# The first weight load gated on one quad's V, and a new order of the steps, in a fused chunk-select attention and feed-forward kernel

## The chip, the cores and the metric

The kernel runs on one core of one Trainium2 chip. Its time is the device time of one execution in microseconds (us), lower is better. A core has TensorE (PE; its weight loads are listed apart as PEld), VectorE (DVE), ScalarE (ACT), GpSimd (POOL) and SyncE (SP, which here only issues DMAs). Each engine runs its own instructions strictly in the order in which the program lists them; they wait for one another through semaphores.

## The reference

Sizes: batch 4, 8 heads, 768 positions, head dimension 64; then 3072 tokens of width 512 into a hidden width of 2048. Cut to what matters:

```python
def _attn_ref(q, k, v):
    # chunks of 32 keys; top 6 chunks per query, causal
    k_min, k_max = k_chunks.min(axis=3), k_chunks.max(axis=3)
    ub = sum(maximum(q * k_min, q * k_max), axis=-1)        # per query and chunk
    ub = where(causal, ub, -1e9)
    top_chunks = argsort(ub)[..., -6:]
    scores = scale * (q @ k.T)
    scores = where(key's chunk in top_chunks and key <= query, scores, -1e9)
    return softmax(scores) @ v

def _moe_ref(x, w_in, w_out):
    h = x @ w_in
    g = h * clip(h + 3, 0, 6) / 6
    return g @ w_out
```

## The kernel before

**Tiling.** The heads go in pairs: p0 to p15, four pairs to a batch, two pairs to a quad. Quad 0 of batch 0 is p0 and p1, quad 1 is p2 and p3. A unit is a quad and a half of the 768 queries: u0 (quad 0, first half), u1 (quad 1, first half), u2 and u3 (the second halves) for batch 0; u4 to u7 for batch 1, and so on. When all four pairs of a batch have a half done, that half (384 tokens, a group: g00, g01, g10, ...) goes through the feed-forward part.

**Steps of a unit.** `turn` brings K and Q of a pair to a layout with the head dimension on partitions: on PE for batch 0 (L418, with `turn_out` that evicts it, L291 on ACT or L293 on DVE), on DVE for later batches (L430). `limits` takes maximum and minimum of each chunk on DVE (L443, L444) and their difference on POOL or DVE (L446). `bounds` multiplies them with the queries on PE (L499, tile UBT). On DVE follow `bounds_in` (L503), `largest` (L515), `select` (L520, L523) and `select_out` (L528, tile MT: the mask). `scores` (PE, L556 in batch 0, L559 later, tile SPS), `exponentials` (ACT, L569, tile PT), `triangle` (POOL, L574), `values` (PE, L590, tile PVP) and `values_out` (DVE, L596 and L602, tile Xb) are the attention proper. `cast_values` turns V into bf16 (tile VB from VS).

**Steps of a group.** `turn_tokens` (PE, L611) and `turn_tokens_out` (DVE, L615) for batch 0; then 16 times `hidden` (PE, L647, four matmuls of 384 columns from WIN into HP), `hidden_relu` (ACT, L652) and `hidden_out` (DVE, L655); then three times four `result` steps (PE, L662, four matmuls of 512 columns from WOUT into OP), `result_scale` and the store. Parts 0 and 1 of a result read the first half of WOUT, parts 2 and 3 the second. The last result of the kernel is split (L671). A hidden, a bounds or a result takes one of four PSUM banks (kind "m").

**Loads.** Q, K and V of batch 0 come by SP in pieces (`load_quad`, L266; `load_quad_values(n, part)`, L281, three parts for each of the units 0 to 3, into VS: units 0 and 2 hold quad 0's V, units 1 and 3 quad 1's). Batch 1's K and Q come as four pieces each (`load`, L275). The weights come by POOL in four pieces of 1 MB in bf16, in this order: WIN first half, WIN second half, WOUT first half, WOUT second half (L359, L362). Ahead of each, POOL copies a few elements of another tile ("seen", L356), which makes it wait until that tile has landed: the first for V, the second for the first half of WIN, the third for K of unit 4, the fourth for the second half of WIN.

**Order.** `Plan` holds all 1666 steps (an instruction group on one engine, or a DMA's landing), with lengths and dependencies. `ORDER` is a written-out list that gives each step a rank. `Plan.order` replays the steps with its own lengths, and whenever an engine is free it takes the ready step of lowest rank for which there is room; that yields each engine's program order. Steps that may run on two or three engines go to the one that would finish them sooner. Where the replay sees PE idle over 0.3 us in the first 45 us, it puts dummy matmuls ahead of the next step (L243).

Of the kernel before, what the change touches and what calls it, by code (L numbers as in the profile page):

```python
# [24 lines left out]


ORDER = [int(n) for n in """
# [43 lines left out]
""".split()]  # L71


# [126 lines left out]
def kernel(  # L200
# [575 lines left out]
    landing = {}  # L776
# [172 lines left out]
    for what in ("I0", "I1", "O0", "O1"):  # L949
        name, n = dict(I="WIN", O="WOUT")[what[0]], int(what[1])  # L950
        if what == "I0":
            got, seen = sum([landing["V%d" % i][0] for i in range(4)], []), lambda: VS[0:1, :, :, 3, 0]
        else:
            got, seen = landing[GATE[what]]
            got = got[-1:]
# [96 lines left out]
```

## Time and profile before

| | |
|---|---|
| median of 3 runs | 264.02 us (263.66 to 264.3) |
| profiled execution, own time | 264.45 us |
| its span (first to last instruction) | 262.7 us |
| time outside the span | 1.75 us |
| PE busy in the span | 257.8 us (98%) |
| DVE, ACT, POOL busy | 199.8, 186.5, 133.7 us |

The span starts at 0; all times of events below count from there. Busy time of an engine is the union of its instructions' durations; matmuls overlap in the pipeline, so the distance between starts, not the duration of one, tells how fast they are fed. A bracket at the end of a timeline row gives the engine's idle time before it and what ended it.

### The profile page before, as it was taken

Reading aid. Unit: us, or ns where it says so; the run is one execution under the profiler, and the core shown is the slowest. Engines: PE = TensorE matmul, PEld = TensorE weight load, DVE = VectorE, ACT = ScalarE, POOL = GpSimd, SP = SyncE. Lnnn points to the kernel's source line nnn. Section 1 sums busy time; section 2 is a strip of 40 time slices with the busy share of each in tenths; the row PEclk is TensorE's granted clock in tenths of the full one; section 3 lists DMA queues with packets and bytes.
Section 4 is the critical chain, followed back from the end, with each engine's and each line's share of the span. In section 5 each row is a group of like instructions: output and inputs, shape, how many; then the busy total and the mean of one; then the engine's idle time right before and its main releaser. Section 6 shows DMA issues by size and latency. Waiting matters only on the chain.

```text
span 262.7 us, 6919 instructions
## 1 busy us (share of the span) xinstructions
PE 257.8 (98%) x2544; PEld 157.1 (60%) x2544; DVE 199.8 (76%) x569; ACT 186.5 (71%) x310; POOL 133.7 (51%) x307
## 2 busy tenths in 40 slices
PE   8999999999999999999999999999999999999995
PEld 7865666664545676654666566544665576545543
DVE  5999898999998899989996999879584136804710
ACT  4599889794646799962999768823998297806812
POOL 6538699714956788692762999702533121200000
PEclk9999999999999999999999999999999999999999
DMA  7998999998738899935999993204403021302112
GB/s 205 326 216 125 194 158 216 137 183 154 204 100 161 178 202 144 244 111 157 176 183 209 198 222 145 60 2 116 125 20 105 0 80 48 117 2 80 40 42 80
DMA packets 117986, 35.91 MB, mean 137 GB/s; under 512 B 101184, under 2 KB 113728, under 8 KB 117952
## 3 DMA queue, kind: packets, MB, share of 16 engines
q1 hardware_dynamic: 114400, 30.98, 52.5%
q0 software_dynamic: 3136, 4.19, 10.2%
q8 instruction: 20, 0.33, 0.5%
q10 hardware_dynamic: 416, 0.30, 0.3%
q14 instruction: 14, 0.11, 0.1%
HBM read 29.23 MB, written 8.26 MB: 143 GB/s over the span
## 4 chain that ended last, share of the span: by engine, by line
PE 90%; DVE 6%; ACT 1%; DMA 1%; issue 1%; ACTq 0%; DVEq 0%
PE HP L647 32%; PE OP L662 30%; PE SPS L559 11%; PE PVP L590 8%; PE UBT L499 3%; PE SPS L556 2%; PE KT L418 1%; PE OP L671 1%; ACT PT L569 1%; DMA KS<-in_k_dram 1%; DVE KMA L443 1%; DVE KMA L444 1%; DVE T L515 1%; DVE MT L528 1%; PE QT L418 1%
## 5 line engine op out<-in xcount | busy, mean ns | idle before, releaser
L569 ACT ACTIVATE PT<-SPS 128x1024 bf16<-128x1024 f32 (+2 forms) x96 | 85.6, 935 | 21.7 <-PE SPS L559 18.8
L647 PE MATMUL HP<-XT,WIN 128*128 128x384 bf16 x512 | 90.7, 326 | 0.0
L655 DVE SCALAR_TENSOR_TENSOR GT<-U,HP 128x384 bf16<-128x384 bf16 x128 | 67.6, 548 | 24.9 <-ACT U L652 20.2
L662 PE MATMUL OP<-WOUT,GT 128*128 128x512 bf16 x368 | 85.7, 379 | 0.0
L652 ACT ACTIVATE U<-HP,THREE 128x384 bf16<-128x384 f32 x128 | 72.7, 600 | 12.0 <-PE HP L647 7.9
L647 PEld LDWEIGHTS <-WIN 128*128 128x128 bf16 x512 | 48.4, 98 | 30.1 <-issue 0.8
L662 PEld LDWEIGHTS <-GT 128*128 128x128 bf16 x368 | 35.0, 98 | 38.8 <-issue 2.2
L574 POOL TENSOR_SCALAR_AFFINE_SELECT PT<-PT 128x256 bf16<-128x256 bf16 x96 | 38.4, 410 | 37.1 <-ACT PT L569 35.7
L559 PE MATMUL SPS<-QLA,KL 128*128 128x384 bf16 (+2 forms) x240 | 35.8, 278 | 0.0
L374 POOL TENSOR_SCALAR_AFFINE_SELECT QLA<-QF 64x384 bf16<-64x384 f32 x48 | 24.1, 506 | 19.8 <-PE SPS L559 13.2
L689 ACT ACTIVATE OT<-OP 128x512 f32<-128x512 f32 x22 | 13.1, 597 | 25.1 <-PE OP L662 24.9
L559 PEld LDWEIGHTS <-KL 128*128 128x128 bf16 x240 | 21.6, 98 | 12.8 <-issue 0.5
L374 POOL TENSOR_SCALAR_AFFINE_SELECT KL<-KF 64x384 bf16<-64x384 f32 x48 | 24.1, 504 | 9.9 <-DVE KF L430 8.0
L590 PEld LDWEIGHTS <-PT 128*128 128x128 bf16 x672 | 24.0, 97 | 4.3 <-issue 0.6
L590 PE MATMUL PVP<-VB,PT 128*128 128x65 bf16 x672 | 25.6, 193 | 0.0
L602 DVE TENSOR_TENSOR Xb<-PVP,RINV 128x384 bf16<-128x384 f32 x32 | 18.5, 579 | 1.1
L596 DVE RECIPROCAL RINV<-PVP 128x6 f32<-128x6 f32 x32 | 5.8, 182 | 15.8 <-PE PVP L590 15.8
L640 POOL COPY XT<-BF 128x384 bf16<-128x384 bf16 x20 | 9.4, 509 | 15.6 <-DMA BF<-BD 15.3
L457 ACT ACTIVATE QR<-QF 128x384 f32<-128x384 f32 (+1 forms) x28 | 13.1, 489 | 5.9 <-DVE QF L430 5.8
L430 DVE STREAM_TRANSPOSE QF<-QS 128x384 f32<-128x384 f32 x24 | 12.9, 558 | 1.2 <-PE UBT L499 1.2
L443 DVE TENSOR_REDUCE KMA<-KF 128x12 f32<-128x384 f32 x24 | 13.0, 542 | 0.3
L444 DVE TENSOR_REDUCE KMA<-KF 128x12 f32<-128x384 f32 x24 | 13.0, 543 | 0.0
(81 smaller groups left out, 237.2 us busy)
## 6 DMA issues: line engine op xcount, KB each, us to landing
KS<-in_k_dram SPq DMA_DIRECT2D x31, 192.0 KB, 3.9
QS<-in_q_dram SPq DMA_DIRECT2D x31, 192.0 KB, 4.0
out_dram<-OT SPq DMA_DIRECT2D x20, 256.0 KB, 2.6
VT<-in_v_dram SPq DMA_DIRECT2D x24, 192.0 KB, 3.6
QLA<-MT SPq DMA_DIRECT2D x22, 96.0 KB, 2.2
WIN<-in_moe_w_in_dram POOLq DMA_DIRECT2D x2, 1024.0 KB, 9.6
WOUT<-in_moe_w_out_dram POOLq DMA_DIRECT2D x2, 1024.0 KB, 12.4
BD<-BT SPq DMA_DIRECT2D x5, 384.0 KB, 2.3
```

Of the source, the lines that this page charges most:

```text
L374: nc.gpsimd.affine_select(out=to, in_=x, pattern=[[0, n]], compare_op=A.is_ge, fill=0.0, base=0, channel_multiplier=0)
L443: nc.vector.tensor_reduce(out=over, in_=chunks, axis=X_AXIS, op=A.max)
L444: nc.vector.tensor_reduce(out=low, in_=chunks, axis=X_AXIS, op=A.min)
L559: nc.tensor.matmul(SP[:, j, c0:c0 + n], lhsT=KLS[st["pair"] % 6][:, j, jb * P:(jb + 1) * P], rhs=st["QL", half][:, j, at:at + n], start=Tr ...
L569: nc.scalar.activation(PT[:, :, 0:cols], SP[:, :, 0:cols], ACT.Exp, scale=scale)
L574: nc.gpsimd.affine_select(out=PT[:, :, c0:c0 + P], in_=PT[:, :, c0:c0 + P], pattern=[[0, 2], [1, P]], compare_op=A.is_ge, fill=0.0, base=0 ...
L590: nc.tensor.matmul(PVP[:, j, n, :], lhsT=PT[:, j, c0:c0 + P], rhs=st["VB"][:, jb, j, :], start=(jb == 0), stop=(jb == qb))
L602: nc.vector.tensor_tensor(out=to, in0=PVP[:, :, :, 0:D], in1=RINV[:].to_broadcast([P, 2, HB, D]), op=A.mult)
L647: nc.tensor.matmul(HP[:], lhsT=WIN[:, kt, f * P:(f + 1) * P], rhs=g["XT"][:, kt, :, :], start=(kt == 0), stop=(kt == KT_HID - 1))
L652: nc.scalar.activation(U[:], g["HP", f][:], ACT.Relu, bias=THREE[:], scale=1.0)
L655: nc.vector.scalar_tensor_tensor(out=g["GT"][:, f, :], in0=g["U", f][:], scalar=6.0, in1=g["HP", f][:], op0=A.min, op1=A.mult)
L662: nc.tensor.matmul(g["OP", t][:], lhsT=g["GT"][:, f, t * P:(t + 1) * P], rhs=WOUT[:, f, :], start=(f == 0), stop=(f == FT - 1))
```

## The change

The gate of the first weight load: it waited for all twelve landings of V of batch 0 and read one element of each of the twelve pieces; now it waits for the six landings of quad 1's V (units 1 and 3) and reads six elements. And `ORDER` is replaced by another permutation of the same 1666 steps. The steps themselves, their instructions, their sizes, `SEQ`, the other gates and the replay are the same.

```diff
 ORDER = [int(n) for n in """
-0 21 1 17 2 31 57 58 3 5 53 59 56 54 25 55 4 7 22 67 9 60 63 18 61 11 68 32 69 13 62 6 71 15 64 167 66 65 26 70 19 169 72 8 171 168 73 23 76 10 33 170 74 75 12 80 35 172
-77 174 14 47 173 16 84 49 81 93 78 43 94 85 95 186 79 96 20 97 86 82 24 83 88 194 37 87 34 39 98 91 187 36 89 177 51 90 191 48 99 190 41 175 195 50 27 199 178 115 92 44
...
+0 21 1 17 2 5 57 58 3 47 53 59 56 54 23 55 4 7 22 67 9 60 63 18 61 11 68 6 69 13 62 48 71 19 64 167 66 65 24 70 15 169 72 8 171 168 73 25 76 10 37 170 74 75 12 80 172 39
+77 173 14 49 174 20 78 27 81 93 84 31 94 79 95 186 83 96 16 85 88 82 175 187 26 86 43 191 190 38 176 51 177 97 89 40 87 29 179 194 50 90 91 33 98 178 28 195 180 45 92 182
...
         if what == "I0":
-            got, seen = sum([landing["V%d" % i][0] for i in range(4)], []), lambda: VS[0:1, :, :, 3, 0]
+            got, seen = landing["V1"][0] + landing["V3"][0], lambda: VS[0:1, 1, :, 3, 0]
```

Read with the steps' names, the places in the list (0 to 1665) of the steps that the prediction speaks of are:

| step | engine | place before | place after |
|---|---|---|---|
| last of quad 1's V loads, `load_quad_values(1,2)` | SP | 111, 23rd issue | 95, 20th issue |
| first and last of `load_quad_values(0,..)` | SP | 5, 56 | 69, 113 |
| `load_quad_values(2,2)` | SP | 100 | 117, the last of batch 0 |
| first half of WIN | POOL | 159 | 142 |
| second half of WIN | POOL | 227 | 225 |
| first half of WOUT | POOL | 250 | 289 |
| second half of WOUT | POOL | 338 | 353 |
| `bounds(u2)` | PE | 135 | 125 |
| `limits(p2,1)`, `limits(p3,1)` | DVE | 143, 182 | 165, 174 |
| `values_out(p0,0)` | DVE | 163 | 183 |
| `select_out(u2)` | DVE | 177 | 158 |
| `scores(p0,1,0)` | PE | 187 | 179 |
| `bounds(u3)` | PE | 196 | 195 |
| first `hidden` of g00 | PE | 248 | 247 |
| `triangle(p2,1,3)` | POOL | 288 | 287 |
| `values_out(p2,1)` | DVE | 305 | 310 |
| `turn(p4,QS,0)`, `turn(p5,QS,0)` | DVE | 354, 367 | 314, 320 |
| first step that reads the second half of WOUT | PE | 419, `result(g00,2,2)`, after 86 PE steps | 427, `result(g00,1,2)`, after 87 PE steps |

The 45 PE steps up to and with the two `turn_tokens` of g00 and the two scores behind them are the same set in both lists; only their order among themselves differs.

## Rows read from the trace of the kernel before

**Rows 1.** Page, part 1: busy us and share of the span, by engine.
```profile
PE 257.8 (98%) x2544; PEld 157.1 (60%) x2544; DVE 199.8 (76%) x569; ACT 186.5 (71%) x310; POOL 133.7 (51%) x307
```

**Rows 2.** Windows: stretch, its length, then busy us and instructions by engine, clock, DMA.
```profile
10.00:20.00 10.00, 10.00 (x156) 6.92 (x152) 9.62 (x38) 7.98 (x17) 3.78 (x11) 1.00 1.02 238
20.00:30.00 10.00, 9.37 (x146) 5.35 (x146) 8.80 (x41) 9.04 (x15) 7.41 (x17) 1.00 0.98 157
30.00:40.00 10.00, 9.58 (x154) 6.61 (x150) 9.75 (x22) 8.70 (x12) 8.82 (x20) 1.00 1.07 168
```

**Rows 3.** Chain that ended last, in order of time: start, us, what.
```profile
49.89 10.40 PE HP L647 x64
60.29 3.45 PE OP L662 x16
...
256.39 3.51 PE OP L671 x32
```

**Rows 4.** Timeline of PE, 22 to 36 us: start, us, what, idle before.
```profile
22.46 0.61 PE L243 MATMUL KT<-IDENTB 128*128 128x128 bf16 x8
...
25.78 0.34 PE L556 MATMUL SPS<-MT,EB 64*128 64x384 bf16 x2 [0.57 <-DVE MT L528]
...
26.76 0.85 PE L499 MATMUL UBT<-QF,KMA 64*32 64x384 f32 x8
...
30.56 0.34 PE L556 MATMUL SPS<-MT,EB 64*128 64x384 bf16 x2 [0.30 <-ACT PT L569]
...
35.41 0.82 PE L647 MATMUL HP<-XT,WIN 128*128 128x384 bf16 x4
```

**Rows 5.** Timeline of DVE, 21 to 51 us.
```profile
21.14 0.54 DVE L444 TENSOR_REDUCE KMA<-KT 128x12 f32<-128x384 f32 x1
...
23.38 0.56 DVE L602 TENSOR_TENSOR Xb<-PVP,RINV 128x384 bf16<-128x384 f32 x1
...
25.15 0.58 DVE L528 STREAM_TRANSPOSE MT<-SELA 128x384 bf16<-128x384 bf16 x1
...
28.32 0.58 DVE L503 STREAM_TRANSPOSE UB<-UBT 128x384 f32<-128x384 f32 x1 [0.99 <-PE UBT L499]
...
43.47 0.56 DVE L602 TENSOR_TENSOR Xb<-PVP,RINV 128x384 bf16<-128x384 f32 x1
...
50.90 0.57 DVE L430 STREAM_TRANSPOSE QF<-QS 128x384 f32<-128x384 f32 x1
```

**Rows 6.** Timeline of POOL, 20 to 49 us.
```profile
20.02 0.78 POOL L574 TENSOR_SCALAR_AFFINE_SELECT PT<-PT 128x256 bf16<-128x256 bf16 x2 [0.50 <-ACT PT L569]
...
21.95 0.19 POOL L356 COPY seenWIN<-VS 1x12 f32<-1x12 f32 x1
22.50 1.00 POOL L359 DMA_DIRECT2D WIN<-in_moe_w_in_dram  x1 [0.37 <-issue]
...
35.62 0.91 POOL L362 DMA_DIRECT2D WOUT<-in_moe_w_out_dram  x1
...
41.22 0.40 POOL L574 TENSOR_SCALAR_AFFINE_SELECT PT<-PT 128x256 bf16<-128x256 bf16 x1
...
48.95 0.93 POOL L362 DMA_DIRECT2D WOUT<-in_moe_w_out_dram  x1
```

**Rows 7.** Tiles VS (15.6 us) and QS (32.6 us): issue in ns, us to landing.
```profile
L281 SPq DMA_DIRECT2D VS<-in_v_dram x1: 770/770/770, 15.6 to 15.6; - x1
...
DMA to landing us min/median/max: 5.1/5.1/5.1
...
L275 SPq DMA_DIRECT2D QS<-in_q_dram x1: 857/857/857, 32.6 to 32.6; - x1
...
DMA to landing us min/median/max: 13.0/13.0/13.0
```

**Rows 8.** Tile WIN, 22 to 24 us: landing of the first half.
```profile
DMA to landing us min/median/max: 9.8/9.8/9.8
```

**Rows 9.** Tile WOUT, 48.9 to 50 us: landing of the second half.
```profile
DMA to landing us min/median/max: 12.0/12.0/12.0
```

82 rows, old and new, of the table ORDER are left out of this document.

## The prediction

> **What bounds the kernel now.** I read the page first: PE is busy for 98% of the span, far above the other engines [rows 1]. Matmuls overlap, so that share alone proves little, and I went on to the chain that ended last. From 49.89 us it shows 64 matmuls of HP in 10.40 us, 162 ns apiece, and 16 of OP in 3.45 us, 216 ns apiece [rows 3]. Single HP steps elsewhere in the timeline run at the same distance, so this is PE's own pace and not that of a feeder. The first HP is at 35.41 [rows 4]; from there on there is always feed-forward work to put between attention steps. The last matmuls start at 256.39 and last 3.51 [rows 3], so PE is done at 259.9 of 262.7; the 2.8 us behind it are the last eviction and store, and the change leaves these steps as they are.
>
> A change that alters no step can therefore act in two ways. It can let PE reach its first HP sooner, because the steps that PE does before that are the same set in both lists: the gain is idle PE time removed. Or it can open gaps behind 35.41, where there are hardly any to close. So the gain has a ceiling, which the windows give: PE has 0.63 idle from 20 to 30 us and 0.42 from 30 to 40 [rows 2], and it runs eight dummy matmuls of 0.61 [rows 4], in all 1.66 us. Before 20 us I count nothing: PE's first eight steps keep their places, and from 10 to 20 us PE is busy throughout [rows 2].
>
> **The Trainium skill on this reading.** The page "Perfetto Trace Analysis", section "Identifying the Most-Contended Engine", says that matmul busy share is a poor measure for TensorE and that the weight loads' busy share should be taken. That would be 60% [rows 1], which would leave some 100 us in which a better order could gain anywhere in the kernel. The 162 and 216 ns above speak against that room, so I give it no case.
>
> **The gate.** The first half of WIN is issued at 22.50, behind its copy at 21.95 [rows 6]. The last V landed at 15.6 + 5.1 = 20.7 [rows 7], so it isn't V that holds the copy in the end but POOL's queue: a triangle, a cast and a limit stand ahead of it. With the gate on quad 1, whose last load is now issued three places earlier, at 0.5 to 0.77 per issue [rows 7], V would allow the copy at some 18.4 to 19.2; but the copy still stands behind the triangles of p1, which ran at 20.02 to 20.80 [rows 6]. I expect the issue at 21 to 22, so 1.0 us earlier. The bounds are 0 (the queue decides alone) and 3.5 (21.95 against 18.4, V alone decides). What is that worth? WIN landed at 22.5 + 9.8 = 32.3 [rows 6, 8], and its first reader starts at 35.41. That is 3.1 us of slack, so the gate by itself is worth 0 in either case; the cover is the attention work of batch 0, and if the attention were ready before 32.3 it would be worth up to 1.0. The copy reads six elements instead of twelve: 0.19 us at most, on an engine with slack, 0 on the path.
>
> The Trainium skill's "DMA: Bandwidth & Descriptors", "Rules for kernel authors", advises issuing a DMA early and waiting late. By that rule the first HP would move with the load and give 1.0 us; the row above has it wait for something else, and I take 0.
>
> **The order, before the first HP.** Follow the mask of u2. PE waits 0.57 for it at 25.78 [rows 4], after DVE wrote MT at 25.15 [rows 5], and the dummies before that are also time in which PE had nothing useful. On DVE two things stood ahead of that mask: `limits(p2,1)`, two reductions of 0.54 that overlap a little, 1.0 in all, and `values_out(p0,0)`, 0.56 and a short reciprocal, 0.7 in all [rows 5]. Both are now behind `select_out(u2)`, and `bounds(u2)` stands ahead of the PE steps that it followed. So MT should come about 1.7 us earlier, at some 24.0 in place of 25.7 for its end, and PE needn't wait there.
>
> What is late next is `bounds(u3)`, which needs the limits of p3. DVE goes from 24.0 through `limits(p2,1)` and `limits(p3,1)`, 2 x 1.0, to 26.0, and POOL's difference takes some 0.35 with its semaphore: 26.35. Before, it started at 26.76 [rows 4]. That is 0.41 us gained. DVE's idle 0.99 at 28.32, while it waits for that step [rows 5], is then partly filled by the moved `values_out`. Behind it PE waits 0.30 for ACT [rows 4], and the windows leave about as much in small gaps up to 40 us. The exponentials of p0's second half can now start some 1.5 us sooner, so I take half of these 0.7, 0.35. The sum is 0.41 + 0.35 = 0.76, rounded to 0.75. Its bounds are 0 (ACT, at 9.04 of 10 us in this stretch [rows 2], was as binding as DVE) and the ceiling 1.66.
>
> Against its own time: the span goes from 262.7 to 261.95, and with the 1.75 us outside it from 264.45 to 263.7. That execution lies 0.43 above the median of the runs, 264.02, to which I apply the same difference: 263.3.
>
> V of quad 0 is now loaded among the last, so it lands about where quad 1's last did, at 20.7, or an issue later, 21.5. Its casts feed `values(p0,0)`, which stood just before the dummies of 22.46 [rows 4] and goes behind p3's scores, to about 23.6. That leaves 2 us for the casts, one instruction per pair and half, so I cost it at 0; without that cover PE would wait some tenths.
>
> **The order, after the first HP.** WOUT's first half is issued later: it was at 35.62, and now follows the triangle that ran at 41.22 [rows 6], so about 40.9. Its first reader is at about 60; with the 12.0 us that WOUT's second half took [rows 9] it lands at 53, hidden by some 7 us of PE's work. The second half goes behind three `queries` steps of about 0.53 and loses one or two steps ahead of it: net some 0.5 later on POOL, less the 0.75 gained. I keep 49 for the issue and 61.0 for the landing [rows 6, 9]. Its first reader came two result steps (2 x 0.865) behind the first at 60.29 [rows 3], at 62.0; one more step of 0.865 stands ahead now, less 0.75: 62.1. Slack 1.1.
>
> **The rivals.** *Nothing moves.* ACT or POOL binds where DVE did, or the dummies are simply put elsewhere. For it: ACT is busier than DVE from 20 to 30 us [rows 2]. Against it: PE's longest wait there is ended by DVE. It gives 264.0, and so does the case that the gate has no effect and the order merely shuffles.
>
> *Slower: Q of batch 1 comes late to DVE.* `turn(p4,QS,0)` ran at 50.90; it now follows `values_out(p2,1)`, which ended at 43.47 + 0.56 = 44.0, so DVE reaches it at 43.3. It needs all four Q pieces of unit 4, and the last landed at 32.6 + 13.0 = 45.6 [rows 5, 7]. If that doesn't improve, DVE stands for 2.3 us with the `hidden_out` steps queued behind it, each of which holds one of four banks; PE's lead of one or two steps of 0.65 covers up to 1.0, and PE loses about 1.3 or more: 264.6 to 265.6, with 264.8 as its middle. Against it: the fourth piece flew beside WIN's second half and, from 35.62, WOUT's first half as well; with WOUT out of the way until 40.9 it should land soon after WIN's second half, at 41 to 43. It decides from a landing at about 44.3 on. A late WOUT second half would have a similar price: each us beyond its slack of 1.1 stands on PE.
>
> *More.* All idle time goes, dummies too: 262.4.
>
> **How the numbers follow.** This kernel's runs spread by about 0.2%, 0.5 us, and less can't be told from no change. Forecast (0.4 to 1.2 gained and kept, 262.8 to 263.6): 0.44. Nothing moves (263.6 to 264.5): 0.28. Late Q or late WOUT: 0.17. All idle time: 0.06. A gap that the new order opens somewhere behind 65 us, where I followed no step, about 265: 0.05. Faster: 0.41 of the forecast, of which the lowest gains don't count, and 0.06, in all 0.47. Same: 0.28, and 0.03 from the forecast's edge, less 0.03 from the two slow cases' mildest: 0.28. Slower: 0.25. The range runs from the ceiling, 262.3, to 265.2, which leaves out the worst of the late cases; the forecast's own range is 262.8 to 263.6.
>
> **What would show it.** Right: WIN's first issue at 21 to 22 us; MT of u2 at about 24 with no PE wait for it; `bounds(u3)` near 26.35; first HP near 34.65; from there PE at 162 and 216 ns to the end. Wrong: the first HP at 35.4 or later (the order gained nothing), or DVE idle ahead of a QF transpose at about 43 to 46 or PE idle ahead of OP near 62, ended by a DMA, or PE gaps between batches.

## The result and the profile after

The changed kernel takes 267.75 us (median of 4 runs, 267.29 to 268.03) against 264.14 (4 runs, 263.66 to 264.3) on the same chip: ratio 1.0138, interval 1.0118 to 1.0158. It is 1.4% slower; the forecast was 263.3 with a range of 262.3 to 265.2, so the time lies 2.55 us beyond the range. Its profiled execution took 267.66, with a span of 265.9 where before had 262.7. Two far slower executions, one of e5 at 445.66 us and one of the kernel before at 941.11, are left out of every median and ratio below.

I read the page first. After, parts 1, 3 and 6 (queue: packets, MB, share of 16 engines; issues: KB each, median us from issue to landing):

```profile
span 265.9 us, 6900 instructions
...
PE 258.6 (97%) x2540; PEld 157.5 (59%) x2540; DVE 199.0 (75%) x569; ACT 186.8 (70%) x309; POOL 135.7 (51%) x308
...
q1 hardware_dynamic: 114400, 30.98, 65.4%
...
KS<-in_k_dram SPq DMA_DIRECT2D x31, 192.0 KB, 4.8
...
VT<-in_v_dram SPq DMA_DIRECT2D x24, 192.0 KB, 4.5
```

Before, the same parts:

```profile
q1 hardware_dynamic: 114400, 30.98, 52.5%
...
KS<-in_k_dram SPq DMA_DIRECT2D x31, 192.0 KB, 3.9
...
VT<-in_v_dram SPq DMA_DIRECT2D x24, 192.0 KB, 3.6
```

The engines' busy times hardly differ from [rows 1]. What differs is SP's queue, q1: the same 114400 packets and the same 30.98 MB take 65.4% of sixteen engines' 265.9 us in place of 52.5% of 262.7. That is 0.654 x 16 x 265.9 / 114400 = 24.3 ns a packet, before 19.3. The diff has no line about these packets.

Next the stretch that I had forecast, to the first HP. PE after, timeline:

```profile
23.87 0.29 PE L243 MATMUL PVP<-IDENTB 128*128 128x64 bf16 x4
...
24.84 0.34 PE L556 MATMUL SPS<-MT,EB 64*128 64x384 bf16 x2 [0.29 <-ACT PT L569]
...
26.34 0.85 PE L499 MATMUL UBT<-QF,KMA 64*32 64x384 f32 x8
...
30.15 0.34 PE L556 MATMUL SPS<-MT,EB 64*128 64x384 bf16 x2 [0.30 <-ACT PT L569]
...
35.00 1.48 PE L647 MATMUL HP<-XT,WIN 128*128 128x384 bf16 x8
```

POOL after, timeline, the gate and the weights' issues:

```profile
20.75 0.18 POOL L356 COPY seenWIN<-VS 1x6 f32<-1x6 f32 x1
20.88 1.00 POOL L359 DMA_DIRECT2D WIN<-in_moe_w_in_dram  x1
...
41.00 0.93 POOL L362 DMA_DIRECT2D WOUT<-in_moe_w_out_dram  x1
...
48.90 0.92 POOL L362 DMA_DIRECT2D WOUT<-in_moe_w_out_dram  x1
```

The steps went much as forecast: `bounds(u3)` at 26.34 (26.35 forecast, 26.76 in [rows 4]), no wait for a mask at 24.84, WIN's first issue at 20.88 (21 to 22 forecast, 22.50 in [rows 6]), WOUT's second issue at 48.90 (49). The first HP is at 35.00, 0.41 earlier than in [rows 4]. So the loss lies behind it. PE after, 60 to 200 us, waits (engine and line, what was waited for: us in total, times, longest):

```profile
PE SPS L559 <- DMA QLA<-MT: 1.0, 1, 1.0
PE HP L647 <- DVE GT L655: 0.9, 3, 0.5
PE PVP L590 <- DVE GT L655: 0.3, 1, 0.3
PE HP L647 <- POOL XT L640: 0.2, 1, 0.2
```

The same view of before has no row at all. Matmuls overlap, so I go by their starts as well. By the distance between starts, less what the same pair of steps takes elsewhere, I count eight gaps over 0.15 us behind 36 us, in all 3.79: 1.02 from 64 to 70 us, 1.37 from 100 to 114 (most of these end with DVE's GT), 1.08 at 124.4 (the mask copies) and 0.32 at 162.7. Before had one, of 0.19. The account of the span closes: -0.41 + 3.79 - 0.19 = 3.19, measured 3.2.

DVE is where the chain goes on. DVE after, timeline:

```profile
44.01 1.03 DVE L430 STREAM_TRANSPOSE QF<-QS 128x384 f32<-128x384 f32 x2
...
61.30 1.50 DVE L430 STREAM_TRANSPOSE KF<-KS 128x384 f32<-128x384 f32 x3 [1.51 <-DMA KS<-in_k_dram]
...
99.15 0.58 DVE L430 STREAM_TRANSPOSE KF<-KS 128x384 f32<-128x384 f32 x1 [0.99 <-DMA KS<-in_k_dram]
```

Q of unit 4, my rival, is there in time, by 0.3 us: its last piece landed at 43.73, and there is no wait at 44.01. It is K of unit 5 that DVE waits for, 1.51 us at 61.30, and K of unit 9 at 99.15. Behind each stand GT steps, which PE needs. Tile KS after, the two issues under way from 47 to 49 us (how long the issue took in ns, its start, then us from issue to landing, min/median/max):

```profile
L275 SPq DMA_DIRECT2D KS<-in_k_dram x2: 4202/4788/5375, 42.6 to 48.0; - x2
...
DMA to landing us min/median/max: 12.2/12.7/13.2
```

Before, the same stretch:

```profile
L275 SPq DMA_DIRECT2D KS<-in_k_dram x2: 857/2450/4043, 44.3 to 48.4; - x2
...
DMA to landing us min/median/max: 6.5/6.5/6.5
```

The issue of the last piece began 0.4 us earlier, but it took 4.2 us in place of 0.9 and so ended at 52.2 in place of 49.3; the piece landed at 48.0 + 13.2 = 61.2 in place of 48.4 + 6.5, about 55.

### The profile page after: what moved, and what is told of

It is laid out like the page before. It is cut to its first block, busy times and chain, and to the rows that moved or that the text cites. A ratio compares the mean times of both kernels' runs of the same rounds, so it can differ in the third digit from the quotient of the medians.

```text
span 265.9 us, 6900 instructions
## 1 busy us (share of the span) xinstructions
PE 258.6 (97%) x2540; PEld 157.5 (59%) x2540; DVE 199.0 (75%) x569; ACT 186.8 (70%) x309; POOL 135.7 (51%) x308
## 3 DMA queue, kind: packets, MB, share of 16 engines
q1 hardware_dynamic: 114400, 30.98, 65.4%
## 4 chain that ended last, share of the span: by engine, by line
PE 70%; DMA 10%; DVE 6%; SPq 4%; POOL 4%; ACT 2%; issue 2%; DVEq 0%; POOLq 0%; ACTq 0%
PE HP L647 23%; PE OP L662 22%; PE SPS L559 6%; PE PVP L590 5%; DMA KS<-in_k_dram 5%; PE UBT L499 4%; SPq L275 3%; PE SPS L556 3%; PE KT L418 2%; PE QT L418 2%; ACT PT L569 2%; DMA QS<-in_q_dram 2%; DVE KF L430 2%; DVE GT L655 2%; DMA QLA<-MT 1%
## 5 line engine op out<-in xcount | busy, mean ns | idle before, releaser
L569 ACT ACTIVATE PT<-SPS 128x1024 bf16<-128x1024 f32 (+1 forms) x96 | 85.2, 937 | 13.0 <-PE SPS L559 9.6
L640 POOL COPY XT<-BF 128x384 bf16<-128x384 bf16 x20 | 9.3, 505 | 20.8 <-DMA BF<-BD 20.4
L430 DVE STREAM_TRANSPOSE KF<-KS 128x384 f32<-128x384 f32 x24 | 12.8, 558 | 3.2 <-DMA KS<-in_k_dram 3.2
L457 ACT ACTIVATE QR<-QF 128x384 f32<-128x384 f32 (+1 forms) x25 | 11.0, 461 | 5.1 <-DVE QF L430 5.0
```

Source lines behind the costliest of these rows:

```text
L430: nc.vector.transpose(T[:], st[name][:, st["i"], half * HC:(half + 1) * HC, :].rearrange("p c e -> p (c e)"))
L569: nc.scalar.activation(PT[:, :, 0:cols], SP[:, :, 0:cols], ACT.Exp, scale=scale)
```

## The experiments

Theory 1: the new order is to blame; it lets K, Q and V fly beside WOUT (issued at 41.0 in place of 35.6), and longer packets are the sign of that contention. Theory 2: the longer packets belong to the execution or the chip and not to the program. Times below stand against the kernel before on the same chip (medians 263.52 us for e1 to e4, 264.1 for e5 to e8, 264.16 for e9 to e12, 263.83 for e13).

**e1_before_again, e2_after_again** repeat both kernels unchanged, one run each.

> The kernel before, unchanged, for its DMA. In the profile of before a 128-byte packet of SP's queue took 13 ns in the mean, in that of after 19 ns, and SP's queue took 52.5% against 65.4% of the DMA engines' span. Theory 1 (the order makes the waits, and makes the transfers crowd one another): here about 13 ns and 52 to 53%, time about 264. Theory 2 (the chip or its neighbours make the packets slow in these hours, whatever the kernel): 17 to 20 ns here too, and a time of 265 or more.

> The changed kernel once more, on the same chip as the kernel before. Theory 1: 267 to 268 us, PE gaps behind 60 us of some 3.6 us again, packets at about 19 ns. Theory 2: if the packets are at 13 ns this time, the K loads of unit 5 land before 61 us, the gaps shrink and the time is 264 to 265.5.

Before: 264.32 us, q1 52.4%, K 3.9 us to landing. After: 266.56, q1 64.0%, K 5.1, and PE gaps of 3.36, the largest again in front of the scores that wait for the mask copies, at 122 us here. The time is somewhat under the 267 to 268 expected by theory 1, but the long packets are there again with the changed kernel alone. Theory 2 falls.

**e3_gate_only** is the kernel before with the new gate and the old order:

```diff
-            got, seen = sum([landing["V%d" % i][0] for i in range(4)], []), lambda: VS[0:1, :, :, 3, 0]
+            got, seen = landing["V1"][0] + landing["V3"][0], lambda: VS[0:1, 1, :, 3, 0]
```

> The new gate with the old order. In the program POOL's copy keeps its place and only reads six elements in place of twelve. My prediction's step: the gate by itself is worth 0, 264.0 plus or minus 0.3, WIN's first issue still at about 22.5. Rival (V's landing did hold the copy): WIN is issued at 21 or sooner, and the time moves by 0.5 or more in either direction.

265.36 us (265.04 to 266.71), ratio 1.0073 (1.0044 to 1.0102). The page, parts 3 and 6:

```profile
q1 hardware_dynamic: 114400, 30.98, 63.4%
...
KS<-in_k_dram SPq DMA_DIRECT2D x31, 192.0 KB, 5.0
```

Every engine's instructions are those of before in their order, but for a copy of 1x6 in place of 1x12 and one semaphore wait less ahead of it on POOL. WIN's issue came no earlier (22.7 us). And yet the packets are long, with the old order and the old WOUT issues (35.8 and 49.1). Theory 1 does not explain that.

**e4_order_only** is the reverse: the new order with the old gate.

> The new order with the old gate on all of V. The replay then puts the first WIN copy behind two casts and two triangles on POOL, some 1.5 to 2 us later than in the changed kernel. If the order carries the loss: 267 to 268.5 us. If the gate, by starting the weights at 20.9, carries it: 264 to 265.5.

267.59 us (267.22 to 267.94), ratio 1.0143 (1.0124 to 1.0162), but q1 at 51.7% and K at 3.8: no long packet. The 4.13 us of gaps lie elsewhere, some 2.5 of them from 89 to 96 us, ended by the exponentials and the triangles. The replay takes the gate's wait into account, and with another gate the same ranks gave POOL, and behind it every engine, another program. So the kernel doesn't isolate the order, and the sum of e3 and e4 says nothing. It does show that this list of ranks is not good beside every gate.

**Theory 3**, formed on e3: the six-element tile is to blame. The tile that the gate's copy writes shrinks from 48 bytes a partition to 24, of which the allocator makes 64 and 32. Everything allocated behind it moves down by 32 bytes, and the tiles that K, Q and V are loaded into move from a multiple of 256 (95488 for the first) to 95456, which is 96 beyond a multiple of 128.

**e5_after_wide** is the changed kernel with the tile kept at twelve, the copy filling half of it:

```diff
-        seen = const.tile([1, *x.shape[1:]], FP32, name=f"seen{name}{part}")
-        nc.gpsimd.tensor_copy(seen[:], x)
+        wide = name == "WIN" and part == 0
+        seen = const.tile([1, 2, 6] if wide else [1, *x.shape[1:]], FP32, name=f"seen{name}{part}")
+        nc.gpsimd.tensor_copy(seen[:, 0, :] if wide else seen[:], x)
```

> The changed kernel, with the tile of the gate's copy kept at its old size of twelve elements, of which six are written: gate and order are those of the change, but every tile behind it lies where it lay before (K and Q tiles at a multiple of 128 bytes in each partition, not at 96 beyond one). Theory 3 (the smaller tile moved the tiles, and SP's packets to moved tiles take longer): packets of 128 bytes at 13 ns, SP's queue at 52%, no K landing late, and 263.3 to 264.0, so the 0.4 us that the changed kernel gained before its first HP are kept. Theory 1 (the order makes the waits): 267 or more, with the same gaps behind 60 us.

264.57 us (11 runs), ratio 1.0020 (1.0005 to 1.0035): 1.2% of the 1.4% are gone. It is above the 263.3 to 264.0 that theory 3 had expected, though. The page and the timeline of PE:

```profile
q1 hardware_dynamic: 114400, 30.98, 52.0%
...
KS<-in_k_dram SPq DMA_DIRECT2D x31, 192.0 KB, 3.7
```

```profile
121.47 0.85 PE L500 MATMUL UBT<-QR,KMA 64*32 64x384 f32 x16
123.44 0.60 PE L560 MATMUL SPS<-QLA,KL 128*128 128x384 bf16 x4 [1.11 <-DMA QLA<-MT]
```

One gap is left behind 36 us, and that one is the order's own: the tiles lie here as in before.

**e6_before_shift** is the kernel before with an unused tile of 96 bytes behind the constants, so that all that follows moves by 96. **e7_before_src** moves the K, Q and V tiles alone off (the rest by a full 128), **e8_before_rest** all but K, Q and V.

```diff
+    const.tile([P, 24], FP32, name="PAD")                      # e6
+    src_pool.tile([P, 24], FP32, name="PADA", tag="pada")      # e7, with
+    xpool.tile([P, 8], FP32, name="PADB", tag="padb")          # e7
+    xpool.tile([P, 24], FP32, name="PADB", tag="padb")         # e8
```

> The kernel before with an unused tile of 96 bytes at the end of the constants, ahead of the gate's tile: no instruction differs, only the addresses of all tiles behind, which then have the residue that they have in the changed kernel. Theory 3: as with the gate alone, packets at 17 to 19 ns and 265.0 to 266. Theory 1: 264.0, packets at 13 ns.

> The kernel before with the K, Q and V tiles that SP loads from HBM moved by 96 bytes, and all tiles behind them by 128, which keeps the latter's residue. If the DMA's destination is what counts: packets at 17 to 19 ns and 265 to 266, as when all is moved. If it is the engines' operands (transposed tiles, masks, probabilities): 264.0.

> The complement: K, Q and V tiles of SP's loads stay, all tiles behind them are moved by 96 bytes. If the DMA's destination is what counts: packets at 13 ns, 264.0 plus or minus 0.4. If the engines' operands count: 265 to 266.

| kernel | time us | ratio (interval) | q1 | K, us to landing | PE gaps |
|---|---|---|---|---|---|
| e6, all moved by 96 bytes | 265.63 | 1.0053 (1.0035 to 1.0071) | 63.8% | 5.3 | 2.07 |
| e7, K, Q, V by 96 | 266.46 | 1.0064 (1.0036 to 1.0091) | 63.5% | 5.3 | 2.67 |
| e8, the rest by 96 | 263.90 | 0.9997 (0.9977 to 1.0017) | 52.6% | 3.7 | 0.19 |

The pages of e7 and of e8:

```profile
q1 hardware_dynamic: 114400, 30.98, 63.5%
...
KS<-in_k_dram SPq DMA_DIRECT2D x31, 192.0 KB, 5.3
```

```profile
q1 hardware_dynamic: 114400, 30.98, 52.6%
...
KS<-in_k_dram SPq DMA_DIRECT2D x31, 192.0 KB, 3.7
```

The three have 10, 5 and 10 runs. An unused tile costs half a per cent, without any edit of gate or order. It is the place of the loads' destinations that counts; where the engines' other operands lie did not matter. e7 also moves what the engines read from these tiles, but they read it no slower: DVE's transposes of K took 556 ns in the mean (554 before), POOL's casts of V 908 (906).

**e9_mended** is e5 with one step of the list, `scores(p8,0,0)`, put ten places later, behind two result steps (1222 and 1223); the replay answers by shifting further steps of batch 2 on every engine:

```diff
-1243 1220 ... 1249 648 597 647 731 1247 1222 649 598 632 732 624 1223 633 ...
+1243 1220 ... 1249 648 647 731 1247 1222 649 598 632 732 624 1223 597 633 ...
```

> Gate, order and places of the tiles as in the changed kernel with the tile kept at twelve elements, and in ORDER the first scores of p8 ten places later, behind two result steps in place of ahead of them. In that kernel PE stood 1.1 us at 122 us for a mask copy of these scores. If that gap is what is left of the order's price: PE goes on with eight OP matmuls there, and the time is 263.0 to 263.7, which beats the kernel before by 0.2 to 0.4%. If the replay, which shifts other steps of batch 2 in answer, opens another gap: 264 to 265.

263.87 us (12 runs), ratio 0.9977 (0.9958 to 0.9996); q1 52.3%, span 262.3. PE's timeline:

```profile
121.41 0.85 PE L500 MATMUL UBT<-QR,KMA 64*32 64x384 f32 x16
122.42 1.67 PE L663 MATMUL OP<-WOUT,GT 128*128 128x512 bf16 x7 [0.16 <-issue]
123.93 0.60 PE L560 MATMUL SPS<-QLA,KL 128*128 128x384 bf16 x4
```

The two result steps (eight matmuls of OP, of which the trace holds seven) fill the time in which the mask copies land, and the gap is gone. This version beats both kernels, by about the least that can be told here (263.0 to 263.7 had been expected).

**e10_src32, e11_src64** put K, Q and V 32 and 64 bytes beyond a multiple of 256 (pads of 8 and 16 words in place of e7's 24), in the kernel before.

> The kernel before with the K, Q and V tiles moved by 32 bytes (32 beyond a multiple of 128), all tiles behind them by 128. If a place off a multiple of 64 bytes is what makes the packets long: 17 to 19 ns, some 265.5. If only the residue 96 of the changed kernel did it, where a packet of 128 bytes lies three quarters into the next block: 13 ns, 264.

> The same with 64 bytes. If a multiple of 64 bytes suffices: packets at 13 ns, 264. If it must be a multiple of 128: 17 to 19 ns, some 265.5.

One run each: 266.05 us with q1 at 64.6% and K at 5.0; 264.88 with q1 at 63.7% and K at 5.1. Both have the long packets; the time of e11 lies within the spread of the kernel before (263.44 to 265.85) and tells nothing by itself.

**e12_gate_wide** is e3 with the tile kept at twelve (the two edits above together): the gate by itself.

> The new gate with the old order, and the gate's tile kept at twelve elements, so that no tile moves. My prediction's step (the gate alone is worth 0): 264.0 plus or minus 0.3, packets at 13 ns, where the gate with the smaller tile took 265.4. If the gate itself cost something: 265 or more.

263.94 us (10 runs), ratio 0.9988 (0.9971 to 1.0005), K 3.8. The gate is worth nothing that can be told, as forecast. Its page:

```profile
q1 hardware_dynamic: 114400, 30.98, 52.6%
```

**e13_src128** puts K, Q and V 128 bytes beyond a multiple of 256 (a pad of 32 words). It asks what the destination has to meet.

> The kernel before, with every tile from K, Q and V on moved by 128 bytes, so that K, Q and V lie on a multiple of 128 that is no multiple of 256. If what counts is that a destination starts on a multiple of 128 bytes: SP's queue at 52 to 53%, K at 3.7 to 3.9 us and V at 3.5 to 3.6 us from issue to landing, and the time that of the kernel before within 0.2%. If what counts is a packet that runs across a multiple of 256 bytes: K's and Q's packets of 128 bytes never do and stay at 13 ns, V's of 256 bytes all do; SP's queue between 53 and 60%, K and Q as before, V at 4.3 to 4.6 us, and the time up to 0.4% above. If the tile itself has to start on a multiple of 256: SP's queue at 63 to 65%, K at 5.0 to 5.3, the time 0.5 to 0.9% above, as with 96 bytes.

264.4 us (10 runs), ratio 1.0003 (0.9974 to 1.0032). The page:

```profile
q1 hardware_dynamic: 114400, 30.98, 53.9%
...
KS<-in_k_dram SPq DMA_DIRECT2D x31, 192.0 KB, 4.1
```

The medians lie 0.2% apart; the interval holds that and no difference. From the trace's records of the packets, by size: those of 128 bytes, which are K's and Q's of the later batches, take 13.5 ns in the mean (13.3 in before, 18.7 in after); those of 256 bytes, which are V's, 19.1 (18.1 and 22.2). That the tile has to start on a multiple of 256 is out. A multiple of 128 explains nearly all. A small charge for packets that run across a multiple of 256 is possible, 1 ns of the 4 on V's; but K, whose packets cross none here, also took 4.1 us in place of 3.9 (V 3.9 in place of 3.6, under the 4.3 to 4.6 expected if crossing counted), so this run doesn't settle it.

## Why the prediction was wrong

**The step that failed.** "The copy reads six elements instead of twelve: 0.19 us at most, on an engine with slack, 0 on the path." I costed the copy and not the tile that it writes. With it fails the sentence on which the ceiling rested, that a change which alters no step can act in two ways, by a sooner first HP or by gaps that the order opens. There is a third: it can change how long an unaltered step takes. Here 32 bytes less in one tile made SP's packets 26% longer (24.3 against 19.3 ns). Shown by e3 and e12, which differ in that tile's size alone (ratios 1.0073 and 0.9988 to before), by e5, and by e6 and e7 without the change. The price: 0.5 to 0.7% with the old order (e3, e6, e7), about 1.2% with the new one (1.0138 against 1.0020 of e5, some 3.1 us). So of the 4.45 us between forecast and result some 3.1 are the tile's; some 1.1 are the order's own gap at the mask copies, and 0.3 a front that gained less than forecast, both taken up below.

**Whether the new order pays more** for long packets is not settled. By the medians it does (1.2% against 0.5 to 0.7%), but the interval of e7 reaches 0.9%, and no other shift was tried with the new order. The traces show the same chain with both orders. DVE's waits for SP's loads from 36 us on, in after, e7 and e3:

```profile
DVE KF L430 <- DMA KS<-in_k_dram: 3.2, 3, 1.5
```

```profile
DVE KF L432 <- DMA KS<-in_k_dram: 2.9, 4, 1.2
...
DVE QF L432 <- DMA QS<-in_q_dram: 0.9, 2, 0.5
```

```profile
DVE QF L430 <- DMA QS<-in_q_dram: 0.9, 1, 0.9
```

With equally long packets PE's gaps were 3.79 in after, 1.08 of it at the mask copies, 2.67 in e7, and in e3 its profile has a single wait of 0.3. What the place of the tiles did to unit 5's last K in the new order can be read from e5, which has the same program. KS there, the issue under way from 47 to 49 us:

```profile
L275 SPq DMA_DIRECT2D KS<-in_k_dram x1: 4562/4562/4562, 42.5 to 42.5; - x1
...
DMA to landing us min/median/max: 11.1/11.1/11.1
```

This piece landed at 53.6, while in after it was issued at 48.0 and its issue ended at 52.2, behind that of WOUT's second half at 48.90. That half landed at 60.73 and the piece at 61.22. In before, too, the Q whose issue followed WOUT's second half landed 0.5 us behind it (60.97 and 61.43), and the K issued just ahead of it at 55. So in these traces a load that slips behind a half of WOUT stays out about as long as that half, and DVE waited 1.51 us for this one with GT steps behind.

**The front.** Forecast 0.75 sooner for the first HP; 0.41 in this trace. DVE's part came as worked out: `bounds(u3)` 0.42 sooner against 0.41. The 0.35 for ACT's gaps did not: the wait of 0.30 for ACT stands at 30.15 as it did in [rows 4], and another of 0.29 takes the place of the 0.57 for the mask. One trace is a weak witness for a few tenths, though. The ten profiles with the old order here have the first HP at 34.83 to 35.73, mean 35.34; the four with the new order and gate at 34.41, 34.93, 35.00 and 35.00, mean 34.84. So the gain is some 0.5 us.

**The gate.** Right: in after WIN was issued 1.6 us sooner and landed at 20.9 + 9.4 = 30.3, 4.7 us ahead of the first HP, and the gate alone was worth 0 (e12; there the copy keeps its place in POOL's queue, and the issue at 21.59 was 0.9 sooner). The wait moved to POOL's queue, as I had it: the copy at 20.75 follows the triangles of 20.02 to 20.8.

**Q of batch 1 and WOUT.** Neither rival came true. WOUT landed at 52.5 and 60.7 (53 and 61.0 forecast), and no PE step waited for it. The price that I gave to a late load at DVE, 1.3 us on PE for some 2.3 on DVE, was of the right kind, but it was paid for K of units 5 and 9, whose landings I did not follow: 2.39 us of gaps on PE for 3.2 us of waits on DVE.

**A gap behind 65 us**, which I had at "about 265" with a chance of 0.05, is real: 1.19 us by the starts at 122 in e5 (1.11 in its row), 264.57 us. The new list puts `scores(p8,0,0)` straight behind the bounds of batch 2's last units, where its mask copy has yet to land; the chain of after shows the same place:

```profile
122.05 3.78 DMA QLA<-MT
125.83 0.04 issue
125.87 0.60 PE SPS L559 x4
```

It takes back more than the front gained: e5 is 0.2% above before, and 0.23% below once the step is moved (e9).

**PE as the bound** held: in e9 the profile has four waits of PE behind 36 us, of at most 0.2 us, and the kernel takes 263.87, 0.2% from the forecast. What didn't hold was that only the order could open gaps there.

## What to carry to other kernels

Before a change is costed as "the same steps", compare the addresses too: a tile that grows or shrinks moves everything allocated behind it, and an unused tile of the difference, put in or taken out, is the control. Read the DMA queues' share and the issue-to-landing times of untouched loads ahead of the engines: they showed here in one line what the eight gaps downstream only hinted at. A list of ranks goes with the gates that it was found with: with the old gate the new list had 4.13 us of gaps, though no packet was long (e4).

## What the runs showed of the hardware

The destination's offset within the partition set how long SP's loads of K, Q and V from HBM took. At 32, 64 and 96 bytes beyond a multiple of 128, q1's share was 63 to 65%, in place of 52 to 54% on such a multiple, and the packets of 128 bytes took 17.4 to 18.7 ns in the mean in place of 13.3 to 13.5. Their median stayed at 13; 31 to 38% of them took over 16 ns in place of 3 to 5%, and the longest tenth began at 29 to 32 ns in place of 13. So a part of the packets is hit hard, and the rest not.

The Trainium skill ("DMA: Bandwidth & Descriptors", "How a descriptor splits into AXI transactions") says, of what a descriptor fetches, that a transaction has to start on a multiple of 256 bytes, so that what starts elsewhere begins at the multiple below it. If writes at the destination were split at the same places, which the page does not say and no run here shows, half of the packets of 128 bytes would run across a multiple at 32, 64 and 96 and none at 128 (an estimate from that rule). The direction agrees, the share of long packets does not quite: 31 to 38%, and 5% at 128. And every one of V's of 256 bytes would run across one at 128 as well as at the other offsets; but at 128 these rose by 1 ns only, where the other offsets cost 3 to 5.

Nor is the offset all of it. V of batch 0 has a tile of its own, which in the kernel before already lies 96 bytes beyond a multiple of 128, and its packets took 18.8 ns there (12 to 22 us), hardly more than the 17.9 of later, well placed V's (60 to 110 us). What else it takes, and what lengthens a packet inside the DMA engines, stays open.
